# The third conv unit of each super tile placed between the two output turns of its step instead of at the head of the step

## The chip, the cores and the metric

One core of a Trainium2 chip. The metric is the device time of one execution, in microseconds (us); lower is better. A trace of one profiled execution of every kernel was read as well, and because the effects here are tens of nanoseconds (ns) that repeat thirty times, most readings rest on the traces.

## The reference, cut to what matters

```python
x: (8, 4096, 192)      weight: (8 heads, 7 taps)      w_in: (192, 2048)      w_out: (2048, 192)
w   = softmax(weight, axis=-1)
att = causal depthwise convolution of x with 7 taps, one filter per head of 24 channels
h   = att @ w_in                                      # 32768 tokens x 2048
g   = where(h > 0, h, exp(min(h, 0)) - 1)             # ELU
out = g @ w_out                                       # 32768 x 192, float32
```

## The kernel before: what the change and the argument touch

The 32768 tokens are cut into 32 super tiles of 1024, and a super tile into 16 steps, one for each 128 of the 2048 hidden channels. The matrix unit (TensorE) is split into two halves of 64 rows that work side by side. In the code they are `rt` 0 and 1, here the **lower** and the **upper** half; the two groups of 512 tokens are `g` 0 and 1. In each step either half does

- 3 matmuls of `h` (64 rows x 512 tokens, "h"), the lower half for group 0, the upper for group 1, into one PSUM bank each, called the lower and the upper H tile (PSUM is the memory in which TensorE's results add up; this kernel uses 8 banks of it);
- one turn of 4 output matmuls for group 0 and one for group 1, which add to an accumulator (`a`, one bank per group). The upper half's turn waits for the lower half's and the other way round.

Every fourth step or so there is also a conv unit, 2 matmuls per half: four units make `att` for a super tile that comes later. They stand at steps 14, 2, 7 and 9. ScalarE copies their result out of its bank (an eviction, `csb` in the profile); it evicts a finished accumulator too (`osb`). An accumulator opens with the first output matmul of a new sum, in a bank that must be free by then: group 0's at steps 4 and 12, group 1's at steps 0 and 8.

An H tile passes three engines before its bank is free: ScalarE (`exp`), GpSimd (`clip`), VectorE (`max`, result `gT`).

```python
# ScalarE:  E  = exp(H[bank])                 GpSimd:  E = max(min(E, 1), 0)
# VectorE:  gT = max(E - 1, H[bank])          -> the bank is free
```

GpSimd also issues the loads of `x` (it casts to bf16 on the way). Where a load stands among the clips is decided by the rank of a conv unit in ScalarE's order:

```python
X_AT = ((2, 1, 1), (1, 1, 0))        # (conv unit, super tiles ahead, group)
...
for s in range(2, NS):
    for u, ahead, gr in X_AT:
        if s + ahead < NS:
            x_before.setdefault(h_before(("c", CU * s + u)), []).append((s + ahead, gr))
```

The order of TensorE's matmuls comes from a small model at build time: two lists per step, one per half, merged by modelled clocks; and a bank is given to a new tile by the same model.

```python
CONV_AT = (14, 18, 23, 25)           # steps of the four units, relative to the super tile before last
...
def take_bank(what, rt):
    if what not in bank_of:
        b = min(range(NBANK), key=lambda b: freed[b])     # the bank that came free first
        ...
for n in range(LIVE, NP):
    lists = [[], []]
    convs = conv_steps.get(n, [])
    for m in convs:
        lists[0] += c_items(m, 0)
    lists[0] += block_items(n, 0, 0) + block_items(n, 1, 0) + h_items(n, 0)
    lists[1] += h_items(n, 1)
    for m in convs:
        lists[1] += c_items(m, 1)
    lists[1] += block_items(n, 0, 1) + block_items(n, 1, 1)
    emit(lists)
```

So a step reads: lower half conv, turn of group 0, turn of group 1, h; upper half h, conv, turn 0, turn 1.

## Time and profile before

| | before |
|---|---|
| time, median of the first 3 runs (lowest to highest) | 723.38 us (723.37 to 723.71) |
| span of the profiled run | 720.8 us |
| TensorE's share of the chain that ended last | 95% |
| one super tile (period) | 21.845 us |
| the same without any stall (12 steps of 1.308, 4 of 1.516) | 21.76 us |

How to read it: the span is that of one execution in the trace. The period is the distance from the first h of a super tile to the first h of the next, and it is the number to watch, because 27 super tiles in the middle of the run are nearly alike. The prediction shows the lines behind it.

### The profile page before, as it was taken

The page shows a single profiled execution, that of the slowest core. Times are in us where ns is not written, and L with a number is a line of the kernel's source. Part 1 is how long each engine was busy: PE and PEld are TensorE (multiplying, and loading weights), DVE is VectorE, ACT ScalarE, POOL GpSimd, SP SyncE. Part 2 cuts the span into 40 slices and gives each one's busy share as a digit, 9 for nine tenths or more (in the row PEclk, how much of TensorE's full clock was granted, in tenths as well). Part 3 has the DMA queues.
Part 4 walks back from the last instruction along what each step waited for, and adds up shares of the span by engine and source line. Part 5 has one row for each costly group of instructions (what it writes and reads, how often), then busy time and mean ns, then how long its engine had stood idle before and what let it go on. Part 6 is the DMA issues. An engine that isn't in the chain of part 4 may idle for free.

```text
span 720.8 us, 27612 instructions
## 1 busy us (share of the span) xinstructions
PE 714.6 (99%) x11846; PEld 676.0 (94%) x11847; DVE 642.8 (89%) x1048; ACT 678.6 (94%) x1289; POOL 670.1 (93%) x1115
## 2 busy tenths in 40 slices
PE   8999999999999999999999999999999999999998
PEld 4689999999999999999999999999999999999997
DVE  7989898998899988989888989988989989899994
ACT  6999999999999999999999999999999999999994
POOL 9999999999999999999999999999999999999893
PEclk9999999999999999999999999999999999999999
DMA  9655354554254664344553456552535543645212
GB/s 172 92 87 78 64 90 74 95 87 83 54 96 72 88 97 63 73 83 86 87 97 50 84 74 96 86 86 51 96 73 89 94 69 67 92 79 83 71 35 68
DMA packets 132735, 58.75 MB, mean 82 GB/s; under 512 B 98614, under 2 KB 132036, under 8 KB 132612
## 3 DMA queue, kind: packets, MB, share of 16 engines
q1 hardware_dynamic: 88388, 39.32, 23.9%
q0 software_dynamic: 43936, 16.77, 23.1%
q8 instruction: 93, 1.52, 0.9%
q10 hardware_dynamic: 288, 0.88, 0.4%
q14 instruction: 30, 0.25, 0.1%
HBM read 34.63 MB, written 25.46 MB: 83 GB/s over the span
## 4 chain that ended last, share of the span: by engine, by line
PE 95%; POOL 2%; DVE 1%; ACT 1%; issue 0%; DVEq 0%; POOLq 0%
PE H L1026 54%; PE H L1003 38%; PE H L978 3%; DVE gT L865 1%; POOL w_in L638 1%; ACT E L749 1%; POOL xg L618 0%; POOL w_out L649 0%; ACT csb L745 0%; POOL E L702 0%; POOL owner L666 0%; ACT osb L756 0%; DVE osb L856 0%; POOL block L676 0%; POOL ident L655 0%
## 5 line engine op out<-in xcount | busy, mean ns | idle before, releaser
L865 DVE SCALAR_TENSOR_TENSOR gT<-E,H 128x512 f16<-128x512 f32 x1024 | 633.0, 683 | 64.1 <-POOL E L702 62.4
L1026 PE MATMUL H<-w_out,gT 64*128 64x192 f16 x8192 | 682.2, 243 | 0.1
L1003 PE MATMUL H<-att,w_in 64*128 64x512 bf16 x3072 | 680.3, 376 | 0.6 <-DVE gT L865 0.4
L1026 PEld LDWEIGHTS H<-w_out,gT 64*128 64x128 f16 x8192 | 625.9, 94 | 22.3 <-PE H L1026 1.6
L702 POOL TENSOR_SCALAR E<-E 128x512 f32<-128x512 f32 x1024 | 607.6, 615 | 38.4 <-ACT E L749 28.2
L749 ACT ACTIVATE E<-H 128x512 f32<-128x512 f32 x1024 | 593.1, 602 | 26.5 <-PE H L1003 1.6
L1003 PEld LDWEIGHTS H<-att,w_in 64*128 64x128 bf16 x3072 | 275.2, 93 | 7.9 <-issue 1.2
L978 PE MATMUL H<-xg,Tm 64*128 64x240 bf16 x496 | 91.2, 263 | 0.2 <-DVE gT L865 0.2
L745 ACT ACTIVATE csb<-H 112x480 bf16<-112x480 f32 x124 | 70.1, 565 | 0.1
L756 ACT ACTIVATE osb<-H 128x384 f32<-128x384 f32 (+1 forms) x129 | 62.2, 484 | 6.8 <-PE H L1026 6.8
L618 POOL DMA_DIRECT2D xg<-in_x_dram x62 | 55.4, 898 | 0.2 <-issue 0.2
L978 PEld LDWEIGHTS H<-xg,Tm 64*128 64x128 bf16 x496 | 43.7, 94 | 4.7 <-DVE gT L865 1.1
L856 DVE COPY osb<-H 128x192 f32<-128x192 f32 x1 | 0.4, 358 | 7.3 <-PE H L1026 7.3
L900 PE MATMUL H<-zw 128*128 128x512 bf16 x10 | 4.0, 555 | 1.2 <-DVE zw L764 1.2
L638 POOL DMA_DIRECT2D w_in<-in_moe_w_in_dram x9 | 5.2, 617 | 0.0
L724 ACT ACTIVATE xb<-xs 128x512 bf16<-128x512 f32 x3 | 1.7, 622 | 2.4 <-DMA xs<-in_x_dram 2.4
L954 PE MATMUL H<-xT,taps 128*128 128x256 bf16 (+1 forms) x23 | 3.7, 314 | 0.2 <-issue 0.2
L900 PEld LDWEIGHTS H<-zw 128*128 128x128 bf16 x10 | 1.1, 128 | 2.8 <-issue 1.4
L954 PEld LDWEIGHTS H<-xT,taps 128*128 128x128 bf16 x24 | 2.2, 97 | 1.5
L649 POOL DMA_DIRECT2D w_out<-in_moe_w_out_dram x3 | 2.6, 916 | 0.0
L717 ACT ACT_TABLE_LOAD x1 | 1.3, 1283 | 1.2 <-PEq L1093 1.2
L730 ACT ACTIVATE w_in<-w_in 64x1536 bf16<-64x1536 bf16 (+1 forms) x2 | 2.3, 1164 | 0.0
(43 smaller groups left out, 19.9 us busy)
## 6 DMA issues: line engine op xcount, KB each, us to landing
out_dram<-osb SPq DMA_DIRECT2D x126, 192.0 KB, 3.5
xg<-in_x_dram POOLq DMA_DIRECT2D x61, 240.0 KB, 5.0
xs<-in_x_dram ACTq DMA_DIRECT2D x1, 768.0 KB, 4.6
att<-csb SPq DMA_TRANSPOSE x31, 4.6
w_in<-in_moe_w_in_dram POOLq DMA_DIRECT2D x6, 64.0 KB, 3.0
w_in<-in_moe_w_in_dram POOLq DMA_DIRECT2D x3, 128.0 KB, 5.4
w_out<-in_moe_w_out_dram POOLq DMA_DIRECT2D x2, 192.0 KB, 9.1
w_out<-in_moe_w_out_dram POOLq DMA_DIRECT2D x1, 384.0 KB, 11.9
```

The costliest lines, as they stand in the source:

```text
L618: g.dma_start(xg[0:rows, b, 2 * w0 + gr : 2 * w1 : 2, :], src).then_inc(s_x[b][gr], 16)
L638: g.dma_start(w_in[0:HP, j, c0:c1], bass.AP(tensor=moe_w_in.tensor, offset=8 * j * FF + c0, ap=[[CPH * FF, HEADS], [FF, 8], [1, c1 - c0]], ...
L702: g.tensor_scalar(out=E[:, i % NE, :], in0=E[:, i % NE, :], scalar1=1.0, scalar2=0.0, op0=ALU.min, op1=ALU.max,).then_inc(s_clp)
L745: a.activation(*conv_evac(W, m), ACT.Copy).then_inc(s_ce)
L749: a.activation(E[:, i % NE, :], H[:, bank_of[item], :], ACT.Exp).then_inc(s_exp)
L756: a.activation(*out_evac(W, *item[1:]), ACT.Copy).then_inc(s_oev[item[2]])
L865: v.scalar_tensor_tensor(out=gT[:, s % NG3, q, u, :], in0=E[:, i % NE, :], scalar=1.0, in1=H[:, bank_of[item], :], op0=ALU.subtract, op1=A ...
L900: pe.matmul(H[:, bank, :], zw[:, 0:P], zw[:, 0:GS], start=True, stop=True)
L954: ins = pe.matmul(H[:, bank_of[item] + half, c0:c1], taps[:, tap, :], xT[:, j, HALO - PAD + tap + c0 : HALO - PAD + tap + c1], start=(tap ...
L978: ins = pe.matmul(H[:, bank_of["c", m], 256 * q : 256 * q + UC], Tm[rows, h, :], xg[rows, s % NXB, :, CPH * h : CPH * (h + 1)].rearrange(" ...
L1003: ins = pe.matmul(H[:, bank_of[item[:3]], :], w_in[HP * r : HP * (r + 1), j, FC * q : FC * (q + 1)], att[HP * r : HP * (r + 1), s % 2, j, ...
L1026: ins = pe.matmul(acc_of(k, g)[:, D * kb : D * (kb + 1)], gT[HP * rt : HP * (rt + 1), t % NG3, q, g, t0 : t0 + P], w_out[HP * rt : HP * (r ...
```

## The change

Intent: the third conv unit stands at the head of step 7, where its PSUM bank is only just coming free. Place it between the two turns instead, 330 ns later, and the wait should be over by then.

```diff
 CONV_AT = (14, 18, 23, 25)
+CONV_POS = ((0, 0), (0, 0), (4, 4), (0, 0))
...
-        lists = [[], []]
-        convs = conv_steps.get(n, [])
-        for m in convs:
-            lists[0] += c_items(m, 0)
-        lists[0] += block_items(n, 0, 0) + block_items(n, 1, 0) + h_items(n, 0)
-        lists[1] += h_items(n, 1)
-        for m in convs:
-            lists[1] += c_items(m, 1)
-        lists[1] += block_items(n, 0, 1) + block_items(n, 1, 1)
+        blocks = [[block_items(n, g, rt) for g in range(2)] for rt in range(2)]
+        lists = [sum(blocks[0], []) + h_items(n, 0), h_items(n, 1) + sum(blocks[1], [])]
+        for m in conv_steps.get(n, []):
+            for rt, later in enumerate(CONV_POS[m % CU]):
+                later += 3 * rt
+                lists[rt][later:later] = c_items(m, rt)
```

`(4, 4)` puts the unit behind the four matmuls of the first turn in either half; `3 * rt` allows for the three h with which the upper half's list begins. No instruction is added or removed.

## The prediction

> **What bounds the kernel now.** I read the page first, then periods, then single waits.
>
> ```profile
> PE 714.6 (99%) x11846; PEld 676.0 (94%) x11847; DVE 642.8 (89%) x1048; ACT 678.6 (94%) x1289; POOL 670.1 (93%) x1115
> PE 95%; POOL 2%; DVE 1%; ACT 1%; issue 0%; DVEq 0%; POOLq 0%
> L978 PE MATMUL H<-xg,Tm 64*128 64x240 bf16 x496 | 91.2, 263 | 0.2 <-DVE gT L865 0.2
> ```
>
> The chain that ended last is TensorE for 95% of the span: this is a stream of matmuls with few holes, and L978, the convolution that is moved, is a small part. So the question is not how much work there is, but which holes there are and who makes them. Next, the busy time over two super tiles (1024 tokens each):
>
> ```profile
> 284.64:306.48 21.84, 21.84 (x371) 21.21 (x368) 19.75 (x33) 21.05 (x41) 20.68 (x35) 1.00 0.48 81
> 306.48:328.33 21.85, 21.85 (x372) 21.19 (x368) 19.75 (x33) 21.07 (x41) 20.70 (x35) 1.00 0.46 80
> ```
>
> The period is 21.845 us. A super tile has 16 steps. In each, either row half of TensorE does 3 matmuls of H=att*w_in ("h") and 8 of the output (two turns of 4, group 0 then group 1); four steps also have a conv unit, 2 matmuls per half. I laid the 11,760 matmul records of these three kinds beside the kernel's own order and took start-to-start times per half: 216 ns for an h, 82.5 for an output matmul, 102.5 for a conv matmul, within 1 ns nearly everywhere. An undisturbed step is 3 x 216 + 8 x 82.5 = 1308 ns, one with a conv 1513 (1516 measured). Twelve and four make 21.76 us. So **at most 0.09 us per super tile is lost** in steady state, and 30 times 0.09 = 2.7 us, 0.4%, is all that any reordering there can win.
>
> Where are the 90 ns? In every super tile in steps 7 to 10. Step lengths (first h of the upper half to the next): 1517, 1342, 1560, 1318 for steps 7 (conv), 8, 9 (conv), 10, against 1516, 1308, 1516, 1308. In the super tile whose step 7 starts at 303.55 us three weight loads come late:
>
> ```profile
> 303.46 0.09 PEld L1003 LDWEIGHTS H<-att,w_in 64*128 64x128 bf16 x1
> 303.61 0.09 PEld L978 LDWEIGHTS H<-xg,Tm 64*128 64x128 bf16 x1
> ...
> 305.22 0.38 PEld L1026 LDWEIGHTS H<-w_out,gT 64*128 64x128 f16 x3
> 305.51 0.09 PEld L1003 LDWEIGHTS H<-att,w_in 64*128 64x128 bf16 x1
> ...
> 307.59 0.31 PEld L1026 LDWEIGHTS H<-w_out,gT 64*128 64x128 f16 x4
> 307.96 0.09 PEld L1003 LDWEIGHTS H<-att,w_in 64*128 64x128 bf16 x1
> ```
>
> (1) 303.61: the third conv unit waits for its PSUM bank; the VectorE row that frees it ends at 303.55. Lower half: 44 + 11 ns. (2) 305.50 (joined into the 305.22 row): group 1's new accumulation opens in the bank which that conv unit left, and its ScalarE eviction (304.88 to 305.45) has just ended. Lower half 42 + 10 ns, upper half 20 + 10 + 4 ns. (3) 307.96: the upper half's first h of step 10 waits for a bank freed by VectorE at 307.91. 42 + 10 ns. Each load follows its releaser by 50 to 54 ns. The change touches (1) and (2). What is behind (3)?
>
> ```profile
> 304.39 0.60 ACT L749 ACTIVATE E<-H 128x512 f32<-128x512 f32 x1
> 305.07 0.61 POOL L702 TENSOR_SCALAR E<-E 128x512 f32<-128x512 f32 x1
> 305.63 0.89 POOL L618 DMA_DIRECT2D xg<-in_x_dram  x1
> 306.56 0.63 POOL L702 TENSOR_SCALAR E<-E 128x512 f32<-128x512 f32 x1
> 307.22 0.69 DVE L865 SCALAR_TENSOR_TENSOR gT<-E,H 128x512 f16<-128x512 f32 x1 [0.68 <-POOL E L702]
> ```
>
> A closed chain. The upper half's last h of step 7 starts 0.43 us after the step begins (303.98), whatever else is in the step; ScalarE takes it 412 ns later, its shortest lag in the whole run, so it waits only for TensorE; GpSimd 83 ns after; then GpSimd issues an xg load for 0.9 us, only then clips step 7's other H tile, VectorE finishes that at 307.91, and its bank is the one step 10 opens with. From the start of step 7 to the first h of step 10 that is 4.419 us, and 1516 + 1308 + 1516 = 4340: the chain is **79 ns longer than TensorE's own work**. With 10 ns after it, that is the whole loss of 90.
>
> **What the Trainium skill says.** "TensorEngine Tiling (Array Packing)", Tiling Modes, Key Properties: different tiles can load weights and multiply in parallel. The trace agrees: each half keeps its own spacing, and 55 ns lost by one alone leaves step 7 at 1517. "TensorE: Matmul & The Clock Gate", Part 3, The mechanism: weight loads are pulled ahead where the row group differs, and matmuls start strictly in program order. The first agrees; the second does not: h of step 8 starts at 305.06, before two output matmuls (305.13, 305.22) ahead of it in program order. But wait (2) holds back both halves. "Perfetto Trace Analysis", DMA Instruction - SWDGE (GPSIMD): descriptors are generated on GpSimd's processors, and the record ends when they are done. It agrees: the next clip starts 40 ns after the 0.89 us issue.
>
> **The change part by part.** Same instructions and counts. Running only the kernel's ordering code for both versions: ScalarE, VectorE, GpSimd and the DMA queues keep their order; on TensorE 30 conv units (super tiles 2 to 31) stand one turn, 4 x 82.5 = 330 ns, later in either half; and two banks swap: group 1's opening takes the bank of step 6's upper H tile, and the lower H tile of step 8 takes the conv's. Wait (3)'s bank is not swapped. By hand from 303.55 = 0, in ns, with the lower half 20 behind as now:
>
> - Step 7. The conv's bank is usable at 60, and it is now due at 20 + 330 = 350: wait (1) goes, 55 ns for the lower half. Both halves run unbroken, 1516.
> - The conv's last matmul starts at about 1083 instead of 754. ScalarE's shortest lag for a conv is 299, so its eviction starts at 1382 instead of 1339 (now it queues behind the exponential). Everything queued on ScalarE behind it shifts by 45; GpSimd doesn't feel it, as it is issuing its load until 2.97 us and the shifted tile would be ready at 2.52.
> - Step 8. The opening's bank was released by VectorE at 1799, usable at 1853; due at 1863 less some 80 for the hidden weight load. It stalls by 0 to 10 instead of 52, and the upper half not at all: 1308 instead of 1342, so 34 ns won by then.
> - Step 9. The fourth conv unit takes the bank of group 1's old sum. That eviction ends 45 later, at 2817; the load comes at 2867, the matmul at 2872, but the lower half is now there at 2850: a new stall of some 25 + 10 ns in the lower half alone.
> - Step 10. The upper half arrives at 1516 + 1308 + 1516 = 4340 and waits until 4419, because its chain is the same to the nanosecond. It stalls 79 instead of 42. **The 34 ns are given back**; the lower half simply ends up some 30 ns ahead instead of 40 behind, and waits at the opening of the next super tile.
>
> Sum per super tile: 0 ns, 21.845 us again. Two places lack the chain. In the last super tile with convs but no load left to issue, step 8's 35 ns stay won. In start-up the conv's wait is larger (345 ns lower, 136 upper) and delays the exponential before the same GpSimd load; GpSimd idles 53 ns there, and its backlog allows no more to be won. 0.05 + 0.04 = 0.09 us: 723.38 - 0.09 = 723.3.
>
> **The rivals.** *All 90 ns go*: 30 x 0.09 = 2.7 us, 720.7. For it: the change removes two waits of three, and one might think (3) is their echo. Against it: (3)'s load comes 54 ns after a VectorE end that goes back to step 7's beginning. *New waits cost more*: the later eviction pushes ScalarE (94% busy), the fourth conv's bank comes later still, and rows of TensorE in the new order block each other; 50 to 100 ns per super tile is 1.5 to 3 us, 725 to 726. Against it: the new lateness is 45 ns and falls on the lower half, which has about 80 ns to spare. *The loads move*: GpSimd's xg load is placed by the conv's rank among ScalarE's work; if that rank had changed, chain (3) would start elsewhere. It has not.
>
> **Range and chances.** The three runs of before spread by 0.34 us; one profiled super tile took 0.25 us extra (22.10) by chance. If the walk holds, 723.0 to 723.7; I widen to 722.4 to 724.2 for a misjudged 20 to 30 ns per super tile either way. A gain over 2% would need 14 us, five times all loss there is: 1%. A loss over 2% needs 480 ns per super tile: 1%. Within 2%: 98%.
>
> **What would show it.** Right: periods of 21.84 to 21.85 us, no late weight load at the conv of step 7, step 8 at 1308, but step 10's first h still about 4.42 us after step 7's start, 54 ns after VectorE; the fourth conv's load 50 ns after an osb eviction. Wrong: a period under 21.80 (then (3) was an echo), or over 21.88 (then a stall of the lower half reaches the upper one, or ScalarE's shift reaches GpSimd).

## The result, and the profile after

| | before | after |
|---|---|---|
| time, median of 6 runs (lowest to highest) | 723.40 us (722.63 to 723.71) | 722.94 us (722.40 to 724.25) |
| ratio of the fast runs (95% interval) | | 0.9997 (0.9984 to 1.001) |
| span of the profiled run | 720.8 us | 721.5 us |
| period, median of 27 super tiles | 21.846 us | 21.840 us |
| steps 7, 8, 9, 10 | 1517, 1342, 1560, 1318 ns | 1516, 1307, 1593, 1317 ns |
| first h of step 10 after the start of step 7 | 4.420 us | 4.416 us |

A ratio here and below is the mean time of one kernel's fast runs over that of the other's in the same rounds, so not quite the ratio of the medians quoted. The time is the same within the noise.

Two super tiles of the changed kernel, busy time by engine (columns: the stretch in us, its length, then busy us and instructions of PE, PEld, DVE, ACT, POOL, the granted clock, the share of DMA, GB/s):

```profile
294.33:316.17 21.84, 21.84 (x373) 21.51 (x371) 19.71 (x33) 21.03 (x41) 20.62 (x35) 1.00 0.44 81
316.17:338.01 21.84, 21.84 (x373) 21.43 (x371) 19.73 (x33) 21.02 (x41) 20.72 (x36) 1.00 0.46 80
```

The period is that of before. Now the same super tile as in the prediction; its step 7 starts at 303.69 here. Source lines are two lower than before (L976 is the conv, L1001 h, L1024 the output). TensorE's weight loads (start, length, what, how many in a row):

```profile
303.90 0.09 PEld L1001 LDWEIGHTS H<-att,w_in 64*128 64x128 bf16 x1
303.92 0.18 PEld L976 LDWEIGHTS H<-xg,Tm 64*128 64x128 bf16 x2
...
305.27 0.35 PEld L1024 LDWEIGHTS H<-w_out,gT 64*128 64x128 f16 x3
305.54 0.09 PEld L1001 LDWEIGHTS H<-att,w_in 64*128 64x128 bf16 x1
305.55 0.28 PEld L1024 LDWEIGHTS H<-w_out,gT 64*128 64x128 f16 x4
...
307.66 0.09 PEld L1001 LDWEIGHTS H<-att,w_in 64*128 64x128 bf16 x1
307.70 0.48 PEld L1024 LDWEIGHTS H<-w_out,gT 64*128 64x128 f16 x5
308.10 0.11 PEld L1001 LDWEIGHTS H<-att,w_in 64*128 64x128 bf16 x2
```

The conv's load at 303.92 follows the one before it directly: wait (1) is gone. The load of group 1's opening comes at 305.53 (the last of the three joined into the 305.27 row) and delays only the lower half. But from 307.66 to 308.10 no h is loaded again, because of the chain on the other engines:

```profile
304.53 0.60 ACT L747 ACTIVATE E<-H 128x512 f32<-128x512 f32 x1
305.07 0.57 ACT L743 ACTIVATE csb<-H 112x480 bf16<-112x480 f32 x1
305.21 0.61 POOL L700 TENSOR_SCALAR E<-E 128x512 f32<-128x512 f32 x1
305.77 0.89 POOL L616 DMA_DIRECT2D xg<-in_x_dram  x1
306.70 0.62 POOL L700 TENSOR_SCALAR E<-E 128x512 f32<-128x512 f32 x1
307.36 1.29 DVE L863 SCALAR_TENSOR_TENSOR gT<-E,H 128x512 f16<-128x512 f32 x2 [0.68 <-POOL E L700]
```

Counted from the start of step 7 these are the times of before to a few ns: GpSimd's load at 2.08, the delayed clip at 3.01, VectorE at 3.67 with its first row done at 4.36, and step 10's first h at 4.416. Later are only the conv's eviction (csb), at 1.38 instead of 1.34, and the exponentials behind it: that of step 7's lower tile ends at 2.44 instead of 2.39, while GpSimd is still at its load.

One super tile tests the theory without an experiment. The last of these loads (at step 471, if the steps are counted through from 0 to 511) covers four windows of the input instead of five. On GpSimd, in the changed kernel:

```profile
654.65 0.61 POOL L700 TENSOR_SCALAR E<-E 128x512 f32<-128x512 f32 x1
655.21 0.78 POOL L616 DMA_DIRECT2D xg<-in_x_dram  x1
656.02 1.77 POOL L700 TENSOR_SCALAR E<-E 128x512 f32<-128x512 f32 x3
```

The load takes 0.78 us instead of 0.89, so the late clip starts 2.90 us after step 7 instead of 3.01 and the chain is no longer the longer way. There step 10 doesn't stall in either kernel, and there step 8's gain stays: 21.790 us before, 21.754 after, against 21.845 and 21.840 in the others.

The trace does show something won, if far less than a timed run can: from the first h of step 16 to the first h of step 511 the changed kernel takes 674.75 us, before 675.15. Of the 0.40 us, 0.08 lie in the super tile of start-up, 0.11 in the last three, the rest in 5 ns per super tile and in one odd super tile (see the end). The span is longer all the same, since this run took 0.35 us more before step 16.

### The profile page after: what moved, and what is told of

Its sections match the earlier page's. It is cut to its first block, busy times and chain, and to the rows that moved or that the text cites. A ratio compares the mean times of both kernels' runs of the same rounds, so it can differ in the third digit from the quotient of the medians.

```text
span 721.5 us, 27612 instructions
## 1 busy us (share of the span) xinstructions
PE 715.2 (99%) x11846; PEld 684.3 (95%) x11847; DVE 641.2 (89%) x1048; ACT 677.7 (94%) x1289; POOL 668.1 (93%) x1115
## 4 chain that ended last, share of the span: by engine, by line
PE 94%; DVE 3%; ACT 1%; POOL 1%; issue 0%; ACTq 0%; DVEq 0%
PE H L1024 54%; PE H L1001 36%; PE H L976 4%; DVE gT L863 2%; ACT E L747 1%; POOL E L700 1%; PE H L952 1%; ACT csb L743 0%; PE H L924 0%; PE H L898 0%; ACT L715 0%; POOL xg L616 0%; ACT osb L754 0%; ACTq L712 0%; DVE osb L854 0%
## 5 line engine op out<-in xcount | busy, mean ns | idle before, releaser
L1001 PE MATMUL H<-att,w_in 64*128 64x512 bf16 x3072 | 686.8, 376 | 0.4 <-DVE gT L863 0.2
L1024 PE MATMUL H<-w_out,gT 64*128 64x192 f16 x8192 | 686.7, 243 | 0.1
L1024 PEld LDWEIGHTS H<-w_out,gT 64*128 64x128 f16 x8192 | 632.1, 94 | 17.7 <-PE H L1024 1.4
L1001 PEld LDWEIGHTS H<-att,w_in 64*128 64x128 bf16 x3072 | 273.8, 93 | 6.6 <-issue 1.1
L976 PE MATMUL H<-xg,Tm 64*128 64x240 bf16 x496 | 91.2, 263 | 0.2 <-DVE gT L863 0.2
L976 PEld LDWEIGHTS H<-xg,Tm 64*128 64x128 bf16 x496 | 41.9, 94 | 2.2 <-DVE gT L863 0.5
L924 PEld LDWEIGHTS H<-ident,xb 64*64 64x64 bf16 x48 | 1.7, 146 | 0.9 <-ACT xb L722 0.8
```

Source lines behind the costliest of these rows:

```text
L976: ins = pe.matmul(H[:, bank_of["c", m], 256 * q : 256 * q + UC], Tm[rows, h, :], xg[rows, s % NXB, :, CPH * h : CPH * (h + 1)].rearrange(" ...
L1001: ins = pe.matmul(H[:, bank_of[item[:3]], :], w_in[HP * r : HP * (r + 1), j, FC * q : FC * (q + 1)], att[HP * r : HP * (r + 1), s % 2, j, ...
L1024: ins = pe.matmul(acc_of(k, g)[:, D * kb : D * (kb + 1)], gT[HP * rt : HP * (rt + 1), t % NG3, q, g, t0 : t0 + P], w_out[HP * rt : HP * (r ...
```

## The experiments

Two theories. **Closed chain**: step 7's upper H tile sets off exp, clip, the load on GpSimd, the late clip of the lower tile and its VectorE row, and that row frees the bank of step 10's first h; the chain is longer than TensorE's own work between the two points, so whatever is won between them is given back. **Echo**: the stall of step 10 only passes on waits (1) and (2), and something else (TensorE's order, its halves) sets the period. All kernels gave correct results. The first four ran on one chip beside the kernel before (723.17 us), the next four likewise (722.72), the last two likewise (723.17).

| kernel | time, us | ratio to before (95%) | median period, us | step 7 to step 10's first h, us |
|---|---|---|---|---|
| after_old_banks | 723.45 | 1.0004 (0.9991 to 1.0018) | 21.854 | 4.424 |
| after_two_loads | 790.55 | 1.0933 (1.0918 to 1.0948) | 22.71 | 5.284 |
| before_load_later | 728.72 | 1.0075 (1.0062 to 1.0088) | 21.975 | 4.374 |
| after_load_later | 730.36 | 1.0096 (1.0081 to 1.0112) | 22.025 | 4.341 |
| third_end | 730.59 | 1.0108 (1.0095 to 1.0122) | 22.068 | 4.525 |
| fourth_mid | 722.78 | 1.0001 (0.9987 to 1.0014) | 21.849 | 4.417 |
| fourth_step10_third_head | 722.71 | 0.9999 (0.9986 to 1.0011) | 21.801 | 4.167 |
| fourth_step10 | 721.30 | 0.9979 (0.9966 to 0.9993) | 21.754 | 4.131 |
| fourth_step10_zero12 | 720.73 | 0.9970 (0.9958 to 0.9983) | 21.755 | 4.131 |
| after_again | 723.19 | 1.0004 (0.9991 to 1.0018) | 21.840 | 4.415 |

### after_old_banks: take the gain of step 8 away again

```diff
+            if what[0] == "a" and what[2] == 1 and what[1] % 2 and what[1] < 2 * NS - 4:
+                b = bank_of["c", 2 * what[1] + 8]        # in take_bank: the conv unit's bank, as before
```

> The changed kernel with the bank swap undone: group 1's opening in step 8 takes the bank of the (now later) third conv unit again. Closed-chain theory: the opening waits for the conv's eviction, usable at about 2003 ns after the start of step 7 instead of 1853; step 8 grows from 1307 to about 1390 ns, step 9 shrinks from 1592 to about 1510 to 1520, step 10's first h still starts 4416 to 4420 ns after step 7's start, and the period stays 21.84. If the gain of step 8 were not given back but really won, losing it again would cost 80 ns per super tile, 2.5 us on the whole: 725.4.

Steps 7 to 10 took 1516, 1392, 1516, 1311 ns. Step 8 lost 85 ns against the changed kernel, and step 9 got 77 back:

```profile
304.98 0.57 ACT L745 ACTIVATE csb<-H 112x480 bf16<-112x480 f32 x1
305.60 0.09 PEld L1026 LDWEIGHTS H<-w_out,gT 64*128 64x128 f16 x1 [0.29 <-ACT csb L745]
```

The opening now waits for the conv's eviction (the profile names it as what ended 0.29 us of idle time). Together the steps are 4.424 us: TensorE's own way is now 8 ns longer than the chain, so the stall of step 10 is all but gone, and step 8's loss of 85 ns goes with a period only 14 ns longer; most of that is a new stall of 10 ns at step 1, outside the stretch. This is the plainest proof that, up to that margin, a gain or a loss within the closed stretch does not reach the time.

### after_two_loads: double the suspected cost

```diff
-X_AT = ((2, 1, 1), (1, 1, 0))
+X_AT = ((2, 1, 1), (2, 1, 0))
```

> The suspected cost doubled: in the changed kernel the first xg load of each super tile is issued together with the second, between the two clips of step 7. Closed-chain theory: GpSimd clips the lower tile of step 7 about 0.9 us later, step 10's first h starts about 5.3 us after the start of step 7 instead of 4.42, period 22.7 us, about 26 us more on the whole, near 749. Echo theory, or one in which TensorE's own order sets the period: no change beyond 0.1 us per super tile.

Step 10's first h came 5.284 us after the start of step 7, and three super tiles of four took 22.71 us, both as the chain has it: of the 0.88 us that the second load takes, 0.87 came through, so the chain had no slack to speak of. The echo theory is out. The whole time missed by 41 us, for a reason that I had overlooked. Every fourth super tile took 28.0 to 29.4 us. The rows of GpSimd in such a one:

```profile
259.62 1.76 POOL L616 DMA_DIRECT2D xg<-in_x_dram  x2
261.41 0.63 POOL L700 TENSOR_SCALAR E<-E 128x512 f32<-128x512 f32 x1
266.19 0.25 POOL L631 MEMSET xg<- 6x192 bf16 x1 [4.14 <-DMA xg<-in_x_dram]
```

At the edge of a batch GpSimd clears six rows of the tile just loaded, and must wait until the load, now issued late, has landed. Seven such waits are 31.4 us in the list of waits. The seven super tiles took 43 us more than their neighbours. TensorE stood still for 3.4 to 4.6 us in each, 26 us together, and around the end of each pause the trace shows its granted clock at 0.50 for 3.4 or 6.8 us, 34 us together (steps of 1.31 us took up to 2.56 there). At half speed that is some 17 us more, an estimate from these numbers.

### before_load_later and after_load_later: take the load out of the chain

```diff
-                x_before.setdefault(h_before(("c", CU * s + u)), []).append((s + ahead, gr))
+                x_before.setdefault(h_before(("c", CU * s + u)) + gr, []).append((s + ahead, gr))
```

> The kernel before, with GpSimd's second xg load of each super tile issued one clip later (after both H tiles of step 7 are clipped, not between them). Closed-chain theory: step 10's first h no longer waits; step 9 shrinks from 1560 to about 1517 ns and step 10 from 1318 to 1308, but waits (1) and (2) stay, so step 8 stays near 1342; period 21.79 us instead of 21.845, about 1.6 us off the whole, near 721.8. Echo theory (the wait of step 10 is an echo of waits 1 and 2): nothing in waits 1 and 2 changes, so step 10's stall stays and the period stays 21.84.

> The changed kernel with the same later load. Closed-chain theory: step 9 1516 instead of 1592, step 10 1308, step 8 1308; period 21.755 to 21.76 us, 2.4 us off the whole, near 720.6; so with the chain out of the way the moved conv is worth 34 ns per super tile, 1.0 us more than the kernel before with the same later load. If instead the moved conv is worth nothing because its stalls lie in the lower half alone, both kernels with the later load have the same period. Echo theory: 21.84, no gain.

Half of this came as expected and half failed. Steps 7 to 10 were 1516, 1342, 1516, 1308 ns in the first and 1516, 1307, 1517, 1308 in the second, just as the closed chain says: without the load between the two clips step 10 does not wait, and the moved conv is worth 35 ns. But both kernels are slower by 5 to 7 us, which I had not seen coming. Step 11 is 1482 and 1566 ns instead of 1308 (medians). In after_load_later, whose step 7 starts at 307.59:

```profile
309.44 0.59 ACT L747 ACTIVATE E<-H 128x512 f32<-128x512 f32 x1
310.11 0.62 POOL L700 TENSOR_SCALAR E<-E 128x512 f32<-128x512 f32 x1 [0.38 <-ACT E L747]
310.67 0.89 POOL L616 DMA_DIRECT2D xg<-in_x_dram  x1
313.46 1.87 DVE L863 SCALAR_TENSOR_TENSOR gT<-E,H 128x512 f16<-128x512 f32 x3
314.79 0.09 PEld L1024 LDWEIGHTS H<-w_out,gT 64*128 64x128 f16 x1 [0.32 <-DVE gT L863]
```

The load leaves GpSimd late for the next clips, and the lower tile of step 9 is the first whose bank is wanted soon: group 0's accumulator opens in it at step 12. VectorE's second row of those three ends at 314.74; the opening's load comes at 314.79 and holds back both halves. A second closed chain, longer than the first. (Not all of after_load_later's 7 us is the chain: in its profiled run the granted clock was 0.50 for 3.4 us during start-up, and step 16 began 1.6 us later than in before_load_later. The periods are free of that.)

It also turns the change round. Here the moved conv makes the kernel **slower**, 22.025 against 21.975 us, because this chain passes ScalarE at the point where the change delays it: the exponential of step 7's lower tile ends at 2.44 us instead of 2.39, behind the later eviction, and the opening follows at 7.20 instead of 7.15. So the rival "new waits cost more" was not wrong in its mechanism; in the kernel as it stands GpSimd is still busy with its load at that moment and does not notice.

### third_end: the rank of the conv decides where the load stands

```diff
-CONV_POS = ((0, 0), (0, 0), (4, 4), (0, 0))
+CONV_POS = ((0, 0), (0, 0), (8, 8), (0, 0))
```

> The third unit after both turns of step 7 (330 ns later still). Its eviction now comes after the lower tile's exponential in ScalarE's order, and the xg load, which is placed by that rank, moves one clip later by itself. As in after_load_later the backlog should then meet the opening of step 12: period 21.95 to 22.05 us, 727 to 730. If only TensorE's order mattered, 21.84 and 723.

22.068 us and 730.59, both a little over the range. The load moved by itself, step 11 took 1426 ns (median), and there was a second stall that I had not worked out: the bank of the conv, evicted later still, was given to step 9's first h, and step 8 took 1481. 330 ns more of the same edit cost 7 us.

### fourth_mid: the new stall of the fourth unit taken away

```diff
-CONV_POS = ((0, 0), (0, 0), (4, 4), (0, 0))
+CONV_POS = ((0, 0), (0, 0), (4, 4), (4, 4))
```

> The changed kernel with the fourth unit between the turns of step 9 (not step 10). It removes the new 48 ns stall of the lower half at the fourth unit, but step 10's first h still takes the bank of the lower step-7 tile. Closed-chain theory: step 10's first h again starts 4416 to 4420 ns after step 7's start, the period stays 21.84 us, 723. If the fourth unit's stall were what costs, the period would fall by up to 50 ns, 1.5 us.

The stall of 38 + 10 ns at the fourth conv unit is gone, step 10's first h is at 4.417 us, the period 21.849, no shorter than the changed kernel's 21.840. So the stall cost nothing, as predicted: it lay in the lower half alone.

### fourth_step10 and fourth_step10_third_head: give the chain another customer

```diff
-CONV_AT = (14, 18, 23, 25)
-CONV_POS = ((0, 0), (0, 0), (4, 4), (0, 0))
+CONV_AT = (14, 18, 23, 26)
+CONV_POS = ((0, 0), (0, 0), (4, 4), (4, 4))        # third_head: ((0, 0), (0, 0), (0, 0), (4, 4))
```

> The changed kernel with the fourth conv unit moved too, from the head of step 9 to between the turns of step 10. GpSimd's order is unchanged, so the chain through its load still frees the lower step-7 tile's bank about 4415 ns after step 7's start; but that bank now goes to the fourth conv unit, due at 4460, and step 10's first h takes one that is free since about 3050. Closed-chain theory: no stall of step 10 (steps 9 and 10 become 1308 and 1516 ns), the period falls to 21.76 to 21.80 us, 1.5 to 2.4 us off the whole, 720.8 to 721.7. If the period were set elsewhere (echo, or a bank shortage that only moves on to the next taker), 21.84 and 723.2.

> As fourth_step10, but the third unit back at the head of step 7. This asks what the change under study is worth once the chain binds nothing: closed-chain theory: step 8 is 1342 again (opening waits for the conv's eviction, upper half 34 ns), with no chain to hide it, so the period is 30 to 35 ns longer than fourth_step10's, 1.0 us on the whole. If the moved conv is worth nothing by itself, the two have the same period.

GpSimd's order is not touched in either, but for one cast near the end; ScalarE's is, because the fourth unit's eviction comes later. In fourth_step10 (step 7 starts at 302.68) the chain runs on as before, and nobody stands at its end:

```profile
304.76 0.89 POOL L616 DMA_DIRECT2D xg<-in_x_dram  x1
305.69 0.63 POOL L700 TENSOR_SCALAR E<-E 128x512 f32<-128x512 f32 x1
306.36 0.69 DVE L863 SCALAR_TENSOR_TENSOR gT<-E,H 128x512 f16<-128x512 f32 x1 [0.68 <-POOL E L700]
306.73 0.09 PEld L1001 LDWEIGHTS H<-att,w_in 64*128 64x128 bf16 x1
...
307.12 0.18 PEld L976 LDWEIGHTS H<-xg,Tm 64*128 64x128 bf16 x2
```

VectorE frees the bank at 307.05. Step 10's first h has been loaded at 306.73 from another bank, and the fourth conv unit, which gets this one, is due only at 307.12. The period falls to 21.754 us, every step at its undisturbed length; the whole to 721.30, ratio 0.9979.

With the third unit back at the head of step 7 the period is 21.790 to 21.803 us in most super tiles (21.90 in those with the memset of the next section): step 8 takes 1342 ns again, and in about half of the super tiles another 10 ns appear at steps 0 and 1. So **the change under study is worth 36 to 49 ns per super tile (expected 30 to 35), as soon as the chain no longer ends at step 10**, and next to nothing while it does. On the whole that is 1.2 us between the two traces, from step 16 to the last step. The medians differ by 1.4 us, but the intervals of the two ratios overlap, so here too the traces carry the point.

### fourth_step10_zero12, and after_again beside it

```diff
-ZERO_AT = 8
+ZERO_AT = 12        # on top of fourth_step10
```

> fourth_step10 with GpSimd's batch-edge memset (0.25 us, in every fourth super tile) moved from step 8, where it adds to the backlog behind the xg load, to step 12, where GpSimd has caught up. In fourth_step10 seven super tiles took 21.887 us and the others 21.754; if that 0.13 us is the memset in the chain from the load to the opening of step 11, all take 21.754 here, 0.9 us less: 720.3 to 720.6. If it is something else of the batch edge, no change: 721.3.

> The changed kernel again, unchanged, on the same chip as the one above, to set the two and the kernel before side by side: 723.0 to 723.4, period 21.84 us, 0.996 for the ratio of the best version to it.

Seven super tiles of fourth_step10 took 21.887 us; here all but two of the middle ones (21.945 and 21.766) take 21.755 to 21.757. The memset was in the way. 720.73 us, just over the expected range, beside 723.19 for the changed kernel and 723.17 for the kernel before: this version beats both, by 0.3% (ratio to before 0.9970, 0.9958 to 0.9983). The changed kernel, run again, gave a period of 21.840 and 0.39 us less than before from step 16 to the last step, so that small gain repeats in a second trace.

## Why the prediction was right, point by point

- **What bounds it, and the size of the loss.** Right. With all stalls removed the period is 21.754 us (predicted floor 21.76), and no kernel's usual period went below it.
- **The chain behind wait (3).** Right: doubling its cost moved its end by 0.87 us (predicted 0.9), and taking its end away from step 10 removed the stall. It was not identical to the nanosecond: 4.416 against 4.420 us. GpSimd's and VectorE's instructions were 2 to 3 ns shorter in both traces of the changed kernel (mean of the clip 612 against 615, of the VectorE row 681 against 683); why stays open. ScalarE's 412 ns was not quite the shortest lag of the run (one tile in start-up has 404, another 411), but step 7's was 412 or 413 in all super tiles but one, so that reading holds.
- **Wait (1) goes, step 7 stays 1516.** Right.
- **Step 8 at 1308, its opening delayed by 0 to 10 ns in the lower half.** The step is 1307. The lower half's delay was 30 to 53 ns in nearly all super tiles, because it arrives 13 to 38 ns ahead of the upper one, as the walk's last point foresaw, not 20 behind as its first assumed. It cost nothing.
- **A new stall of 25 + 10 ns at the fourth conv.** 34 to 41 + 10, in the lower half alone; fourth_mid shows that it costs nothing.
- **The 34 ns are given back at step 10: stall 79.** 75 + 10, right; and after_old_banks shows it from the other side.
- **0.09 us outside the chain.** The sign was right, the size too small: 0.08 in start-up (predicted 0.05) and 0.11 at the end (0.04). I had counted step 8 once; it counts twice, 35 ns each, because the last load is short (above), and at two later openings, steps 0 and 1 of the last two super tiles, the upper half loses 14 and 17 ns before and nothing after. Why start-up gained 30 ns more than GpSimd's 53 ns of idle time was not followed up. With the 5 ns per super tile this makes 0.4 us instead of 0.09; the median moved by 0.46 us in one set of runs and not at all in the other (723.19 against 723.17), so timed runs can't confirm it.
- **The super tile of 22.10 us.** I called it chance. It is not: the thirteenth super tile takes 0.06 to 0.25 us longer in eleven of the twelve traces (22.10 before, 22.03 after and again in the rerun, 21.945 in the best kernel). In all twelve, GpSimd pauses for 0.20 us ahead of the first load of that super tile, where other loads follow the clip before them without a gap. What it waits for there stays open, and that the pause makes the super tile longer is likely but not shown: in after_load_later the pause is there and the super tile takes no longer.

## What to carry to other kernels

When an edit removes a wait on the busiest engine, look for the next wait after it and ask where its releaser began: if that chain started before the edit and passes other engines, the gain is given back there. Add up the chain and the engine's own work between the same two points; the longer one is the time, and the difference is all that a change inside can win or lose. And in a kernel whose buffers are all in use, moving work also decides who gets which buffer and when a side engine issues its loads: removing waits alone had won nothing, and giving the late buffer to a taker that comes later had by itself shortened the period (21.801 us) but not the measured time (0.9999). The two together won 0.2%, and with the memset out of the way 0.3%.

## What the Trainium skill lacked or had wrong

- "TensorE: Matmul & The Clock Gate", Part 3, The mechanism, says that matmuls start strictly in program order. With two row halves the records show otherwise: in the trace of before an h of step 8 started at 305.06 us, ahead of two output matmuls of the other half (305.13 and 305.22) that stand before it in the program. Within a half, the program's order fits the records.
- "Perfetto Trace Analysis", Identifying the Most-Contended Engine, names, beside the achieved FLOPs, the summed time of the weight loads over the window as the measure of headroom. With two halves, whose loads overlap, it says nothing here: the sum is 34.4 to 34.5 us in a window of 21.84 us before and after, and 34.2 to 34.4 in fourth_step10, which is faster. The busy time of the windows above, which counts overlapping loads once, went the wrong way: 21.2 us before, 21.4 to 21.5 after at the same period, and only 20.4 to 20.7 in fourth_step10.
- "DMA: Bandwidth & Descriptors" gives a first-byte latency of about 1 us for loads issued by GpSimd; what I missed in it is for how long an issue holds GpSimd's own instructions: here 0.88 us from the end of one clip to the start of the next, for 240 KB.
- I found no page with the lags that this argument needed: 50 to 54 ns from the end of a ScalarE or VectorE row to the weight load that it releases, 412 ns from the start of an h (whose own record lasts 0.38 us, with a modelled end) to ScalarE's start on it, 83 ns from ScalarE's end to GpSimd's start.
